# A written order for every operation in place of a planner: attention over memories and a gated feed-forward, one core

## The chip, the cores and the metric

The kernel runs on one core of a Trainium2 chip. A core has five engines with an instruction queue each: TensorE (PE, matrix products; its weight loads are shown apart as PEld), VectorE (DVE), ScalarE (ACT), GpSimd (POOL) and SyncE (SP, which here issues all transfers). Each queue is worked off in its own order; an instruction whose inputs or buffer are not ready holds everything behind it on that engine. The metric is the device time of one execution in microseconds (us).

## The reference

```
a = softmax(phi over seq)                      # batch 8, heads 8, seq 576, 32 memories
k_m = a^T k ; v_m = a^T v                      # 32 x 64 for each head
attn = softmax(q k_m^T / 8) ; y = attn v_m     # the heads of a token side by side: x, 4608 x 512
h = x @ w_in                                   # w_in 512 x 2048
g = h * erf(softplus(h))
out = g @ w_out                                # w_out 2048 x 512
```

Everything is float32, inputs and output.

## The kernel before, in words

The product `attn v_m w_in` is regrouped: `v_m w_in` is made first, per batch and per 256 columns of `w_in` (the tiles `vw` or `wv`), and `h` is then `attn` (the tiles `at`) times that. A step `i` is one of 128 pieces (batch `b`, 128 of the 2048 inner columns). Batches 0 and 1 make `h` with `ffn1` (L850, two halves of 288 tokens a step). Later batches take two steps at once with `quad` (L756, seven products in place of eight, with sums on DVE before and after). `h` comes out in PSUM as tiles `psh` and is copied or summed into SBUF by ACT or DVE: in batch 0 the copies may go to either engine (L864 on DVE, L865 on ACT), as may one of the four in a `quad` (L779 on DVE, L778 on ACT). Then ACT makes softplus (L872) and erf (L877), each after a table load when the function changes. DVE multiplies (L887), and the product is split into a rounded part (L903 on DVE or L904 on ACT) and the rest (L905 on DVE). From the two parts `ffn2` (L935, tile `g`) makes the second products, four groups of 128 tokens for each step, into the accumulators `pso`. The 64 tokens of a batch that are left over go through DRAM and are multiplied for two batches together (L935 into `psr`).

Most products use split operands, three matmuls for one; the first steps use plain float32. The small products of attention (L598 `phi` by `k`, `v`; L652 `q` by `km` and `w_in` by `vm`) use parts of the array. PSUM has four banks for all `psa` and `psh` tiles, and four for `pso`.

At the start the weights arrive packed and are decoded: DVE makes the upper half in place (L485, a CAST), ACT or DVE the lower half (L486 or L488), and DVE merges them (L480). `w_in` is needed for `vw`, `w_out` for the second products. A score tile `sc` goes through DVE and ACT (L798 transposition, L801 maximum, L803 difference, L806 exp, L807 sum, L809, L811, L812) and becomes `at` with L819. All transfers stand in one SP queue: `phiT`, `kv`, `q`, `w` (each packed weight chunk is one transfer), later `wi` and `rest_d`.

What sets the order of the instructions: every operation is recorded as an `Op` with an engine or two (`ways`), a modelled cost, a rank, and the operations that it must follow. `Plan.order()` then runs a small model of the engines. It takes at each moment the operation of lowest rank that can start soonest and whose tiles have room, with the shift of a table `SHIFT` added to some ranks, and chooses the engine where there are two. The result is the order of emission, and so the order in every queue. In the same model PE's waits of over 450 ns are filled with matmuls of zeros (`fill`, L414, tile `idle`) until the first operation of the kind "stop filling", which is the first second product of all:

```
if filling and gap > 450:
    x.fill = int((gap - 200) / (216 if clock.fast else 432))
...
op(PE, mm(DM, True) if exact else 3 * mm(DM, False), rank, gs + [w_key, o], [o], emit,
   kind="stop filling" if k == 0 else None)
```

Of the kernel before, what the change touches and what calls it, by code (L numbers as in the profile page):

```python
# [41 lines left out]
SHIFT = {  # L42
    "at_sums": {
        ("s", 2): 2, ("s", 3): 2,
    },
    "attention": {
        (0,): 12, (2,): 4.5, (3,): 1,
    },
    "decode": {
        ("in", 0): -9, ("in", 1): -10.5, ("in", 2): -12, ("in", 5): -11, ("in", 7): -11, ("out", 2): 11.5,  # L50
        ("out", 3): -14, ("out", 7): -0.5,
    },
    "ffn2_rest": {
        ("s", 0, 2): 5.5, ("s", 10, 2): -5.5, ("s", 12, 2): 3.5, ("s", 6, 2): 2, (7, 0, 2): -14,
    },
    "g_split": {
# [4 lines left out]
    },  # L61
    "memories": {
        (1,): 1.5, (2,): 4,
    },
    "split_wo": {
        (0,): 13, (4,): 4.5, (6,): 6,
    },
    "vw": {
        (0, 4, False): 1.5, (0, 6, False): -9.5, (1, 1, False): 0.5, (1, 5, False): 5, (1, 6, False): -5.5,
    },  # L70
    "vw_sums": {
        ("s", 3): -6.5, (2, 0): 8, (2, 1): 2.5, (2, 3): -1,
    },
}


class Op:
    def __init__(self, ways, rank, kind, nbytes, edge):
        self.ways, self.rank, self.kind, self.nbytes, self.edge = ways, rank, kind, nbytes, edge
        self.engine = next(iter(ways))  # L80
        self.before, self.after, self.tiles, self.placed = set(), [], set(), []
        self.ready = self.start = self.end = 0.0
        self.fill = 0
# [19 lines left out]

class Plan:
# [3 lines left out]
    SIGNAL = 60.0  # L108
    TABLE = 1283.0
    SWITCH = 98.0  # L110
    RELOAD = 170.0
    NEAR = 100.0

    def __init__(self, room, any_order, least, shared):
        self.ops, self.seen = [], {}
        self.room, self.any_order, self.least, self.shared = room, any_order, least, shared
        self.pool_of, self.users, self.turn = {}, {}, {}

    def tile(self, pool, *key):
        self.pool_of[key] = pool  # L120
        self.users[key] = []
        self.turn.setdefault(pool, []).append(key)
        return key

    shift = 0

    def op(self, engine, cost, rank, reads, writes, emit, kind=None, nbytes=0, edge=None, after=(),
           holds=(), other=()):
        x = Op({engine: (cost, emit), **dict(other)}, rank, kind, nbytes, edge)
        x.shift = self.shift  # L130
        x.before.update(after)
        for w, keys in ((False, reads), (True, writes)):
            for k in keys:
                k, part = (k[0], k[1]) if isinstance(k[0], tuple) else (k, None)
                x.tiles.add(k)
# [18 lines left out]
        for k in x.tiles:  # L154
            if k in self.users:
                self.users[k].append(x)
                x.placed.append(k)
        x.placed += [k for k in holds if k not in x.tiles]
# [3 lines left out]
    def order(self):  # L162
        n_wait = {}
        for x in self.ops:
            x.rank += 100 * x.shift
            n_wait[x] = len(x.before)
            for y in x.before:
                y.after.append(x)
        room, turn = dict(self.room), dict.fromkeys(self.turn, 0)
        left = {k: len(u) for k, u in self.users.items()}  # L170
        waiting = {e: [x for x in self.ops if e in x.ways and not n_wait[x]] for e in ENGINES}
        free = dict.fromkeys(ENGINES, 0.0)
        table, at_edge, small = None, True, False
        landed, clock, filling = 2200.0, Clock(), True
        releases, out, now, held = [], [], 0.0, set()

        def fits(x):
            need = {}
            for k in x.placed:
                if k in held:  # L180
                    continue
                p = self.pool_of[k]
                if p not in self.any_order and self.turn[p][turn[p] + need.get(p, 0)] != k:
                    return False
                need[p] = need.get(p, 0) + 1
            if any(room[p] < n for p, n in need.items()):
                return False
            return not any(p in self.least for p in need) or self.shared >= sum(
                max(n, self.room[p] - room[p] + need.get(p, 0)) for p, n in self.least.items())

        def best_way(x):
            return min(x.ways, key=lambda e: max(free[e], x.ready, now) + x.ways[e][0])

        while len(out) < len(self.ops):
            best = None
            for e, xs in waiting.items():
                can = [x for x in xs if fits(x)]
                if e == ACT and not at_edge:
                    can = [x for x in can if x.kind != "exp"]
                can = [x for x in can if len(x.ways) == 1 or best_way(x) == e]  # L200
                if not can:
                    continue
                t0 = max(free[e], now, min(x.ready for x in can))
                near = [x for x in can if x.ready <= t0 + self.NEAR]
                if e == PE and small and any(x.kind == "small" and x.ready <= t0 for x in near):
                    near = [x for x in near if x.kind == "small" and x.ready <= t0]
                x = min(near, key=lambda x: x.rank)
                t = max(free[e], x.ready, now)
                if best is None or t < best[0]:
                    best = (t, x, e)  # L210
            if releases and (best is None or releases[0][0] <= best[0]):
                now, _, p = heapq.heappop(releases)
                room[p] += 1
                continue
            if best is None:
                raise RuntimeError(f"nothing fits after {len(out)} of {len(self.ops)}")
            now, x, e = best
            x.engine, (cost, x.emit) = e, x.ways[e]
            for w in x.ways:
                waiting[w].remove(x)  # L220
            for k in x.placed:
                if k not in held:
                    held.add(k)
                    room[self.pool_of[k]] -= 1
                    turn[self.pool_of[k]] += 1
# [16 lines left out]
            elif e == ACT:  # L242
                if x.kind is not None and x.kind != table:
                    cost += self.TABLE
                    table = x.kind
                if x.edge is not None:
                    at_edge = x.edge
                late = 75.0
            elif e == DVE:
                late = 60.0  # L250
            x.cost = cost
            free[e] = now + cost
            x.start, x.end = now, now + cost + late
            if e == SP:
                begin = max(now + 900, landed)
                landed = begin + x.nbytes / (250 if x.nbytes < 1.2e5 else 340 if begin < 13000 else 385)
                x.end = landed + 900
            out.append(x)
            for y in x.after:
                n_wait[y] -= 1  # L260
                y.ready = max(y.ready, x.end + self.SIGNAL)
                if not n_wait[y]:
                    for w in y.ways:
                        waiting[w].append(y)
            for k in x.tiles:
                if k in left:
                    left[k] -= 1
                    if not left[k]:
                        end = max(u.end for u in self.users[k]) + self.SIGNAL
                        heapq.heappush(releases, (end, len(out) * 16 + len(releases), self.pool_of[k]))  # L270
# [4 lines left out]
def tile_memory_attention_then_erf_softplus_ffn(  # L275
# [12 lines left out]
    P = 128  # L288
# [21 lines left out]
    MOST = {"h": 14, "e": 12, "at": 14, "sc": 4, "phiT": 3, "uv": 3, "dk": 2, "rr": 3}  # L310
    LEAST = {"h": 4, "e": 4, "at": 7, "sc": 3, "phiT": 2, "uv": 1, "dk": 1, "rr": 2}
# [857 lines left out]
```

## Time and profile before

| | |
|---|---|
| three runs | 704.41 us median, 703.42 to 704.54 |
| the profiled execution | 704.14 us, its span 702.3 us |
| PE, PEld, DVE, ACT busy | 691.8, 549.8, 581.8, 541.9 us |
| HBM read and written | 93.2 and 21.0 MB |
| granted PE clock, mean | 0.998 |

A span is the time from the first to the last instruction; the execution is 1.8 us longer. Busy is the time in which an engine has at least one instruction in flight. Matmuls overlap, so PE's spacing is better read from a run of equal matmuls: its length over their count.

### The profile page before, as it was taken

The page shows a single profiled execution, that of the slowest core. Times are in us where ns is not written, and L with a number is a line of the kernel's source. Part 1 is how long each engine was busy: PE and PEld are TensorE (multiplying, and loading weights), DVE is VectorE, ACT ScalarE, POOL GpSimd, SP SyncE. Part 2 cuts the span into 40 slices and gives each one's busy share as a digit, 9 for nine tenths or more (in the row PEclk, how much of TensorE's full clock was granted, in tenths as well). Part 3 has the DMA queues.
Part 4 walks back from the last instruction along what each step waited for, and adds up shares of the span by engine and source line. Part 5 has one row for each costly group of instructions (what it writes and reads, how often), then busy time and mean ns, then how long its engine had stood idle before and what let it go on. Part 6 is the DMA issues. An engine that isn't in the chain of part 4 may idle for free.

```text
span 702.3 us, 13828 instructions
## 1 busy us (share of the span) xinstructions
PE 691.8 (99%) x5204; PEld 549.8 (78%) x5204; DVE 581.8 (83%) x1202; ACT 541.9 (77%) x978; POOL 30.6 (4%) x70
## 2 busy tenths in 40 slices
PE   8999999999999999999999999999999999999997
PEld 3566678778878888888878888788888888888885
DVE  3999999988878889998987997789998898767750
ACT  4689987977777887888878996589987895686831
POOL 0111210000000000000000000000000000011220
PEclk9999999999999999999999999999999999999999
DMA  8999953861736336273634346445321434330002
GB/s 324 415 393 421 378 186 105 289 238 34 256 106 214 102 123 227 76 236 91 250 119 139 99 147 229 128 133 191 117 76 66 122 100 139 98 110 1 1 1 75
DMA packets 71283, 115.07 MB, mean 164 GB/s; under 512 B 38064, under 2 KB 46256, under 8 KB 71216
## 3 DMA queue, kind: packets, MB, share of 16 engines
q1 hardware_dynamic: 71216, 114.18, 47.3%
q8 instruction: 41, 0.67, 0.4%
q14 instruction: 26, 0.21, 0.1%
HBM read 93.19 MB, written 20.97 MB: 163 GB/s over the span
## 4 chain that ended last, share of the span: by engine, by line
PE 90%; DMA 3%; DVE 3%; ACT 2%; SPq 1%; issue 1%; ACTq 0%; DVEq 0%
PE pso L935 48%; PE psh L756 19%; PE psh L850 7%; PE psr L935 6%; PE psa L652 6%; PE psa L598 2%; DMA q<-qT 2%; DMA phiT<-phiT 2%; PE idle L414 1%; DVE sv L677 1%; PE psa L620 0%; ACT wv L403 0%; SPq L442 0%; DVE wv L405 0%; DVE e L887 0%
## 5 line engine op out<-in xcount | busy, mean ns | idle before, releaser
L935 PE MATMUL pso<-wo,g 128*128 128x512 f32 x1440 | 392.6, 395 | 0.0
L935 PEld LDWEIGHTS pso<-wo,g 128*128 128x128 f32 x1440 | 250.4, 188 | 41.7 <-issue 7.3
L756 PEld LDWEIGHTS psh<-at,wv 128*128 128x128 f32 x1008 | 168.6, 188 | 36.5 <-DVE h L677 1.8
L756 PE MATMUL psh<-at,wv 128*128 128x288 f32 x1008 | 190.9, 298 | 1.2 <-ACT g L904 0.4
L872 ACT ACTIVATE e<-h 128x576 f32<-128x576 f32 x128 | 87.0, 685 | 38.8 <-DVE h L677 31.0
L887 DVE TENSOR_TENSOR e<-e,h 128x576 f32<-128x576 f32 x120 | 88.9, 749 | 19.7 <-ACT e L877 19.4
L905 DVE TENSOR_TENSOR g<-e,g 128x576 fp32r<-128x576 f32 x120 | 89.7, 750 | 0.6
L877 ACT ACTIVATE e<-e 128x576 f32<-128x576 f32 x128 | 84.1, 676 | 0.4
L677 DVE TENSOR_TENSOR uv<-uv,psh 128x288 f32<-128x288 f32 x96 | 43.1, 449 | 19.0 <-PE psh L756 15.8
L677 DVE TENSOR_TENSOR h<-uv,psh 128x288 f32<-128x288 f32 x96 | 43.1, 449 | 13.6 <-PE psh L756 13.0
L904 ACT ACTIVATE g<-e 128x576 fp32r<-128x576 f32 x68 | 46.5, 684 | 8.6 <-PE pso L935 4.1
L935 PE MATMUL psr<-wo,rr 128*128 128x512 f32 x192 | 49.5, 393 | 0.0
L850 PE MATMUL psh<-at_hi,vw 128*128 128x288 f32 x224 | 45.1, 306 | 0.8 <-DVE sc L798 0.8
L771 ACT ACTIVATE uv<-psh 128x288 f32<-128x288 f32 x96 | 38.9, 405 | 8.8 <-PE psh L756 8.0
L872 ACT ACT_TABLE_LOAD x33 | 42.3, 1283 | 3.9 <-DVE h L677 3.4
L877 ACT ACT_TABLE_LOAD x33 | 42.3, 1283 | 0.6
L935 PEld LDWEIGHTS psr<-wo,rr 128*128 128x128 f32 x192 | 34.8, 188 | 6.8 <-issue 0.4
L850 PEld LDWEIGHTS psh<-at_hi,vw 128*128 128x128 f32 x224 | 35.0, 188 | 5.9 <-issue 2.1
L914 POOL CAST rr<-g 128x64 fp32r<-128x64 f32 x32 | 14.0, 447 | 579.9 <-DVE g L903 550.6
L652 PE MATMUL psa<-wi,vm 64*32 64x256 f32 x1024 | 37.1, 383 | 0.0
L984 ACT ACTIVATE ot<-pso 128x512 f32<-128x512 f32 x32 | 18.5, 604 | 20.0 <-PE pso L935 19.7
L403 ACT ACTIVATE wv<-sv 128x512 fp32r<-128x512 f32 x48 | 27.8, 624 | 5.6 <-DVE sv L677 5.3
(88 smaller groups left out, 809.8 us busy)
## 6 DMA issues: line engine op xcount, KB each, us to landing
wi<-w_in_d SPq DMA_DIRECT2D x56, 512.0 KB, 4.6
kv<-kv SPq DMA_DIRECT2D x32, 640.0 KB, 9.1
q<-qT SPq DMA_DIRECT2D x16, 576.0 KB, 6.9
out<-ot SPq DMA_DIRECT2D x32, 256.0 KB, 3.5
w<-w_in SPq DMA_DIRECT2D x8, 1023.8 KB, 14.4
w<-w_out SPq DMA_DIRECT2D x8, 1023.8 KB, 13.6
rr<-rest_d SPq DMA_DIRECT2D x28, 256.0 KB, 3.4
rest_d<-g SPq DMA_DIRECT2D x104, 64.0 KB, 1.7
```

The costliest lines, as they stand in the source:

```text
L403: lambda: nc.scalar.activation(get_hi(), get_src(), AF.Identity))
L652: nc.tensor.matmul(out=get(ps[par])[p * M : (p + 1) * M, m * n : (m + 1) * n], lhsT=w[rows, p, :], rhs=get(x)[rows, p, :], start=True, sto ...
L677: op(DVE, on_dve(n) + extra, rank, reads, [o], lambda: nc.vector.tensor_tensor(out=get_o(), in0=get_x(), in1=get_y(), op=kind))
L756: nc.tensor.matmul(out=get(ps[o]), lhsT=lhsT, rhs=rhs, start=(n < 4 and m == 0), stop=(m == 2), skip_group_check=n >= 4)
L771: lambda x=x: nc.scalar.activation(get(uv)[:, x], get(ps[x]), AF.Identity))
L850: nc.tensor.matmul(out=get(ps), lhsT=x[:, g, k % 2 * P : (k % 2 + 1) * P], rhs=y[:, g, :], start=(n + g == 0), stop=(n == len(parts) - 1 a ...
L872: last[:] = [op(ACT, on_act(S), rank, [("h", i)], [e], lambda: nc.scalar.activation(get(e), get(("h", i)), AF.Softplus), kind="softplus", ...
L877: last[:] = [op(ACT, on_act(S), rank, [e], [e], lambda: nc.scalar.activation(get(e), get(e), AF.Erf), kind="erf", edge=edge, after=last)]
L887: op(DVE, on_dve(S), rank, [e, h], [to if i >= FR2 else (t, 0)], lambda: nc.vector.tensor_tensor(out=get(t)[:, 0].bitcast(F32) if i < FR2 ...
L904: other={ACT: (on_act(S), lambda: nc.scalar.activation(get(t)[:, 0], get(e), AF.Identity))})
L905: op(DVE, on_dve(S), rank, [e, (t, 0)], [(t, 1)], lambda: nc.vector.tensor_tensor(out=get(t)[:, 1], in0=get(e), in1=get(t)[:, 0].bitcast(F ...
L935: nc.tensor.matmul(out=o, lhsT=y, rhs=z, start=(start and n == 0), stop=(stop and n == len(parts) - 1))
```

## The change

The planner in `Plan.order()`, its tables of buffers and the table `SHIFT` go. In their place stands a string, `WRITTEN`, that spells 3504 numbers. The operations are recorded as before and sorted by rank. Each number `n` takes the operation at place `n >> 1` of those that are left, on its first or second engine by `n & 1`. The model of times remains only to decide where zeros are put, with three costs changed a little. The zeros no longer end at the first second product: "stop filling" now marks the second products of step 15. Zeros that stand behind the first second product would be added into the accumulator `pso` of batch 0 instead of being written into a tile of their own.

```diff
+WRITTEN = (
+    "KlcAAjCCAkOAIAEjMlGEACAheheAAAACAEEKACAKGACFDBAAAACAMMhIkcUMSiCSheSMhYhWaOMMWMUhUUhSUMAQeAOhEAAiCiCKCAIhahII"
...
+def numbers(text):
+    n = 0
+    for c in text:
+        d = DIGITS.index(c)
+        n = 32 * n + d % 32
+        if d < 32:
+            yield n
+            n = 0
...
     def order(self):
...
-                x = min(near, key=lambda x: x.rank)
-                t = max(free[e], x.ready, now)
...
+        left, out = sorted(self.ops, key=lambda x: x.rank), []
+        free, landed = dict.fromkeys(ENGINES, 0.0), 2200.0
+        clock, filling, small, table = Clock(), True, False, None
+        for n in numbers(WRITTEN):
+            x = left.pop(n >> 1)
+            e = list(x.ways)[n & 1]
+            cost, x.emit = x.ways[e]
+            now = max([free[e]] + [y.end for y in x.before])
...
     def mm(n, exact):
-        return 2 * (2 * n / 2.4 + 2.5) if exact else n / 2.4 + (15.5 if n == DM else 11.7)
+        return 2 * (2 * n / 2.4 + 2.5) if exact else n / 2.4 + (16.2 if n == DM else 12.3)
...
+        o = get(("pso", 0, 0)) if idle[1:] else idle[0] if idle else None
         for _ in range(n):
             nc.tensor.matmul(
-                out=idle[0].rearrange("p (n c) -> p n c", c=P), lhsT=zeros,
-                rhs=zeros.unsqueeze(1).to_broadcast([P, DM // P, P]), start=True, stop=True,
+                out=o.rearrange("p (n c) -> p n c", c=P), lhsT=zeros,
+                rhs=zeros.unsqueeze(1).to_broadcast([P, DM // P, P]),
+                start=not idle[1:], stop=not idle[1:], skip_group_check=len(idle) > 1,
             )
...
-           kind="stop filling" if k == 0 else None)
+           kind="stop filling" if i == NK - 1 else None)
```

The instructions are the same in kind and number but for a few. Copies of `psh` on ACT are 69 instead of 49, and on DVE 43 instead of 63: of the 20 that move, 11 are those of L864 and 9 those of L779. ACT has 64 instead of 68 of the copies of L904 and DVE has 56 instead of 52 of L903. Two of the decodes of L486 go from ACT to DVE (L488). ACT has 86 table loads instead of 84. The matmuls of zeros are 73 instead of 76; 70 of them stand ahead of the first `ffn1` and three behind its first 16 matmuls, and none behind the first second product.

Three places in the queues are shown. The first is SP's queue from its first transfer on. Before:

```order
L433 DMA phiT<-phiT 128x576 x2
L442 DMA kv<-kv 128x1280 x2
L447 DMA q<-qT 128x4x288
L428 DMA w<-w_in 128x4095
L442 DMA kv<-kv 128x1280 x2
L447 DMA q<-qT 128x4x288
L428 DMA w<-w_in 128x4095
L428 DMA w<-w_out 128x4095
L428 DMA w<-w_in 128x4095
L428 DMA w<-w_out 128x4095
```

And now, the lines being those of the changed kernel:

```order
L371 DMA phiT<-phiT 128x576 x2
L380 DMA kv<-kv 128x1280 x2
L385 DMA q<-qT 128x4x288
L366 DMA w<-w_in 128x4095
L385 DMA q<-qT 128x4x288
L366 DMA w<-w_in 128x4095
L380 DMA kv<-kv 128x1280 x2
L366 DMA w<-w_in 128x4095
L366 DMA w<-w_out 128x4095
L366 DMA w<-w_in 128x4095
```

The second pair of `kv` (for `v_m`) went behind the second `q` and the second `w_in`, and the third `w_in` stands ahead of the first `w_out`.

The second place is DVE's queue around the first `at` tile, with numbers that tell the tiles apart (`sc` with two numbers are the two halves of batch 0). Before, the first half's `at` comes first:

```order
L812 TENSOR_TENSOR sc_264<-sc_264,srs_375 128x576
L485 CAST w_124<-w_124 128x1024
L803 TENSOR_TENSOR sc_367<-sc_367,smx_377 128x576
L480 SCALAR_TENSOR_TENSOR wi_398<-w_124 128x1024
L807 TENSOR_REDUCE ssm_401<-sc_367 128x18
L485 CAST w_127<-w_127 128x1024
L485 CAST w_130<-w_130 128x1024
L809 TENSOR_SCALAR ssm_401<-ssm_401 128x18
L480 SCALAR_TENSOR_TENSOR wi_442<-w_130 128x1024
L811 RECIPROCAL srs_445<-ssm_401 128x18
L819 STREAM_TRANSPOSE at_479<-sc_264 128x576
L812 TENSOR_TENSOR sc_367<-sc_367,srs_445 128x576
```

Now the second half's comes first (`sc_292`):

```order
L748 RECIPROCAL srs_306<-ssm_295 128x18
L746 TENSOR_SCALAR ssm_304<-ssm_304 128x18
L418 SCALAR_TENSOR_TENSOR wi_375<-w_103 128x1024
L748 RECIPROCAL srs_379<-ssm_304 128x18
L418 SCALAR_TENSOR_TENSOR wi_381<-w_120 128x1024
L423 CAST w_135<-w_135 128x1024
L749 TENSOR_TENSOR sc_292<-sc_292,srs_379 128x576
L418 SCALAR_TENSOR_TENSOR wi_413<-w_135 128x1024
L756 STREAM_TRANSPOSE at_429<-sc_292 128x576
L749 TENSOR_TENSOR sc_254<-sc_254,srs_306 128x576
L341 TENSOR_TENSOR vw_458<-psa_443,vw_458 128x256
L756 STREAM_TRANSPOSE at_462<-sc_254 128x576
```

The same operations stand ahead of the first `at` in both, but for the CAST of the first `w_out` (`w_127`), which went behind both `at` tiles.

The third place is PE's queue in batch 5, where attention's small products of the next batch stand between the large ones. Before:

```order
L756 MATMUL psh<-at,wv 128x288 x3
L652 MATMUL psa<-q,km_98 32x288 x8
L756 MATMUL psh<-at,wv 128x288 x3
L935 MATMUL pso<-wo,g 128x512 x6
L652 MATMUL psa<-wi,vm_101 32x256 x16
L756 MATMUL psh<-at,wv 128x288 x3
L935 MATMUL pso<-wo,g 128x512 x3
```

Now:

```order
L694 MATMUL psh<-at,wv 128x288 x3
L872 MATMUL pso<-wo,g 128x512 x3
L590 MATMUL psa<-q,km_98 32x288 x8
L590 MATMUL psa<-wi,vm_101 32x256 x16
L694 MATMUL psh<-at,wv 128x288 x3
L872 MATMUL pso<-wo,g 128x512 x3
```

The two blocks of small products became one here; over the whole program they are 48 instead of 49.

## Rows read from the trace of the kernel before

**Rows 1.** The page's first part (busy time, share of the span, instructions) and the granted clock in 40 slices.

```profile
PE 691.8 (99%) x5204; PEld 549.8 (78%) x5204; DVE 581.8 (83%) x1202; ACT 541.9 (77%) x978; POOL 30.6 (4%) x70
PEclk9999999999999999999999999999999999999999
```

**Rows 2.** Busy time in stretches: the stretch, its length, busy time and instructions of each engine, granted clock, DMA share and GB/s.

```profile
14.30:17.60 3.30, 3.30 (x16) 1.37 (x14) 3.27 (x5) 1.80 (x1) 0.00 (x0) 1.00 1.05 394
17.60:19.40 1.80, 1.39 (x81) 1.18 (x81) 1.05 (x2) 1.02 (x3) 0.00 (x0) 1.00 1.04 419
...
31.00:100.00 69.00, 68.03 (x474) 44.88 (x475) 66.32 (x99) 61.56 (x98) 13.84 (x27) 1.00 0.97 367
100.00:703.00 603.00, 595.39 (x4402) 492.07 (x4400) 496.60 (x1069) 465.22 (x855) 13.98 (x32) 1.00 0.40 130
```

**Rows 3.** The chain that ended last, in order of time: start, length, what (x counts matmuls).

```profile
21.82 3.99 PE idle L414 x18
...
31.31 10.97 PE psh L850 x56
...
43.23 1.96 PE pso L935 x4
```

**Rows 4.** What PE waited for, by name, but for the three waits of the first 20 us: total us, times, longest.

```profile
PE pso L935 <- PE psh L850: 1.0, 1, 1.0
PE psh L850 <- DVE sc L798: 0.8, 1, 0.8
PE psh L756 <- ACT g L904: 0.4, 2, 0.2
...
PE psh L756 <- ACT bias L521: 0.3, 1, 0.3
PE psh L756 <- DVE wv L405: 0.3, 1, 0.3
```

**Rows 5.** The page's list of transfers: size of one, median us from issue to landing.

```profile
kv<-kv SPq DMA_DIRECT2D x32, 640.0 KB, 9.1
q<-qT SPq DMA_DIRECT2D x16, 576.0 KB, 6.9
...
w<-w_in SPq DMA_DIRECT2D x8, 1023.8 KB, 14.4
```

**Rows 6.** The first 45 us in order of time: start, length, engine, line, what, and in brackets the idle time before and what ended it.

```profile
13.60 0.85 DVE L798 STREAM_TRANSPOSE sc<-psa 128x288 f32<-128x288 f32 x2 [5.36 <-PE psa L652]
14.31 1.80 ACT L486 ACTIVATE w<-w 128x1024 int32<-128x1024 uint32 x1 [1.55 <-DMA w<-w_in]
...
17.66 1.33 PE L598 MATMUL psa<-kv,phi 116*32 116x64 f32 x80
...
20.54 0.57 ACT L634 ACTIVATE vm<-psa 64x128 f32<-64x128 f32 x2 [0.85 <-PE psa L620]
...
20.87 0.95 PE L652 MATMUL psa<-wi,vm 64*32 64x256 f32 x16
...
26.11 2.47 DVE L485 CAST w<-w 128x1024 f16<-128x1024 bf16 x2
...
27.04 2.49 ACT L486 ACTIVATE w<-w 128x1024 int32<-128x1024 uint32 x2
...
30.03 0.72 DVE L819 STREAM_TRANSPOSE at<-sc 128x576 f32<-128x576 f32 x1
...
31.15 7.92 PE L850 MATMUL psh<-at,vw 128*128 128x288 f32 x32
...
42.38 0.76 DVE L887 TENSOR_TENSOR g<-e,h 128x576 f32<-128x576 f32 x1
```

**Rows 7.** PE alone, in batch 5 and at the end.

```profile
481.60 0.72 PE L652 MATMUL psa<-q,km 64*32 64x288 f32 x16
482.24 0.66 PE L756 MATMUL psh<-at,wv 128*128 128x288 f32 x3
482.75 1.54 PE L935 MATMUL pso<-wo,g 128*128 128x512 f32 x6
484.22 1.09 PE L652 MATMUL psa<-wi,vm 64*32 64x256 f32 x32
485.24 0.67 PE L756 MATMUL psh<-at,wv 128*128 128x288 f32 x3
...
523.06 1.09 PE L652 MATMUL psa<-wi,vm 64*32 64x256 f32 x32
...
524.57 2.34 PE L935 MATMUL pso<-wo,g 128*128 128x512 f32 x9
```

**Rows 8.** Groups by line: count, busy us, mean ns of one, idle before it and what ended that.

```profile
L865 ACT ACTIVATE h<-psh 128x288 f32<-128x288 f32 x17 | 7.0, 413 | 5.3 <-PE psh L850 5.0
...
L872 ACT ACT_TABLE_LOAD x33 | 42.3, 1283 | 3.9 <-DVE h L677 3.4
L486 ACT ACTIVATE w<-w 128x1024 int32<-128x1024 uint32 x13 | 18.4, 1435 | 1.6 <-DMA w<-w_in 1.6
```

**Rows 9.** The last steps: the last copies and splits of `g` on DVE, and PE's last matmuls in the chain.

```profile
670.64 0.45 DVE L677 TENSOR_TENSOR h<-uv,psh 128x288 f32<-128x288 f32 x1
...
677.39 0.76 DVE L905 TENSOR_TENSOR g<-e,g 128x576 fp32r<-128x576 f32 x1
...
684.36 6.18 PE pso L935 x27
```

More of the change, by code (lines that the diff above doesn't have):

```diff
@@ L37, with __init__ @@
 }
[L42 to L56, printed above, removed]
[4 rows of a table removed]
[L61 to L74, printed above, removed]
-class Op:
[L78 to L83, printed above, removed]
+class Op:
+    def __init__(self, ways, rank, kind, nbytes):
+        self.ways, self.rank, self.kind, self.nbytes = ways, rank, kind, nbytes
+        self.before, self.end, self.fill = set(), 0.0, 0
 class Clock:
@@ L101, in to @@
         self.at = t
-class Plan:
[L108 to L114, printed above, removed]
-        self.ops, self.seen = [], {}
[L116 to L130, printed above, removed]
+DIGITS = "ABCDEFGHIJKLMNOPQRSTUVWXYZabcdefghijklmnopqrstuvwxyz0123456789+-"
@@ L131, in op, with __init__ @@
+def numbers(text):
[6 more added lines that the diff above has]
+            n = 0
+class Plan:
+    SIGNAL, TABLE, SWITCH, RELOAD = 60.0, 1283.0, 98.0, 170.0
+    def __init__(self):
+        self.ops, self.seen = [], {}
+    def op(self, engine, cost, rank, reads, writes, emit, kind=None, nbytes=0, after=(), other=()):
+        x = Op({engine: (cost, emit), **dict(other)}, rank, kind, nbytes)
         x.before.update(after)
@@ L162, in order @@
     def order(self):
[L163 to L206, printed above, removed]
-                x = min(near, key=lambda x: x.rank)
-                t = max(free[e], x.ready, now)
[L209 to L225, printed above, removed]
@@ L250, in order @@
                 late = 60.0
-            x.cost = cost
             free[e] = now + cost
-            x.start, x.end = now, now + cost + late
+            x.end = now + cost + late + self.SIGNAL
             if e == SP:
@@ L256, in order @@
                 landed = begin + x.nbytes / (250 if x.nbytes < 1.2e5 else 340 if begin < 13000 else 385)
-                x.end = landed + 900
+                x.end = landed + 900 + self.SIGNAL
             out.append(x)
[L259 to L270, printed above, removed]
+        assert not left
         return out
@@ L363, in tile_ @@
     def tile_(tag, *key, shape=None, dtype=F32, pool=None):
-        key = plan.tile(tag, *key)
         p, s, d = SHAPES.get(tag, (pool, shape, dtype))
         T[key] = lambda: pools[p].tile(
-            s, d, name=key[0], tag=tag if tag not in MOST else p, bufs=2 if tag == "rx" else None)
+            s, d, name=key[0], tag=p if tag in SHARED else tag, bufs=2 if tag == "rx" else None)
         return key
@@ L607, in one_memory @@
         cost = n_g * NC * (220 if b else 110)
-        op(PE, cost, rank, [a] + kvs, [ps], sums, kind="small", holds=[t])
+        op(PE, cost, rank, [a] + kvs, [ps], sums, kind="small")
         for n, g in enumerate(gs):
             rs = ("prs", b, g)
-            op(ACT, on_act(2 * n_x * D, True), rank, [ps, rs], [(t, n)],
+            op(ACT, on_act(2 * n_x * D, True) + 70, rank, [ps, rs], [(t, n)],
                lambda n=n, rs=rs: nc.scalar.activation(
@@ L760, in product @@
             chain[:] = [op(PE, 3 * mm(U, False), rank + (0 if n < 4 else 60) + 0.1 * n,
-               [(w, (m, a_part)) for m in range(2)] + [at_] + ([] if n < 4 else [ps[o]]), [ps[o]], emit,
-               holds=h + [uv] if n == 0 else (), after=chain)]
+               [(w, (m, a_part)) for m in range(2)] + [at_] + ([] if n < 4 else [ps[o]]), [ps[o]], emit, after=chain)]
         def half(r, u):
@@ L948, in emit @@
         def emit():
+            if i == d == 0:
+                idle.extend([None] * (2 - len(idle)))
             w = [wf[k // 2][:, k % 2]] if exact else [get(w_key)[:, x, k % 2] for x in range(2)]
```

126 lines of the change are left out of this document (77 added, 49 removed), and 4 rows, old and new, of the table SHIFT.

## The prediction, made before the changed kernel ran

> **What bounds the kernel now.** I read the busy time first, then the chain of waits, then the stretches, and the order of time at the start and at the end. The busy time shows TensorE at 99%, ScalarE at 77%, VectorE at 83%, and a granted clock of 1.00 (2.4 GHz) in practically every slice [rows 1]. A busy PE need not be a PE at its pace, so I check the spacing: 27 second products late in the program take 6.18 us, 229 ns each [rows 9], where 512 columns at 2.4 GHz are 213 ns. After the first 31 us PE waits by name only 2.8 us in all: 1.0 once, 0.8 once, and five waits of 0.2 or 0.3 [rows 4]. So nearly every microsecond after the start is a matmul that must be made. An order can only move three things: when the large matmuls begin, what PE waits for behind that, and how often it changes between large and small products.
>
> At the start the chain goes through matmuls of zeros; the large products begin at 31.3 us, run 10.97 us, and the first second product comes at 43.23 after a pause of about a microsecond [rows 3]. In those 31 us PE does little that counts; transfers and VectorE set the pace.
>
> By the Trainium skill (Perfetto Trace Analysis, Identifying the Most-Contended Engine) busy matmuls are a bad measure and the share of weight loads is a better one; that share is 78% here [rows 1] and would leave a fifth of the span as headroom. The spacing of 229 ns against 213 bears out much less, some 7%. By the page a new order could win far more than I allow; it is the fourth rival below.
>
> **Part 1: the first large product (-1.55 us).** Two things are moved. On SP the `kv` pair goes behind a `q` and a `w_in`, and the third `w_in` goes ahead of the first `w_out`. The transfers run at about 0.41 MB per us there (394 and 419 GB/s, DMA share over 1) [rows 2], with 1.31 MB for the `kv` pair, 0.59 for `q` and 1.05 for a weight chunk [rows 5]. The `kv` pair comes (0.59 + 1.05)/0.41 = 4.0 us later than at 17.66 [rows 6], at 21.7. The third `w_in` comes 1.05/0.41 = 2.6 us earlier than at 27.04 [rows 6], at 24.5. On ACT its decode now stands between the `kvk` and the `vm` copies.
>
> The path by `vm`: the decode takes 24.5 to 25.9 (1.44 us [rows 8]); the copies of `vm` follow, and the first product by `w_in` comes 0.33 us after they start (20.54 to 20.87 [rows 6]), at 26.2. Two blocks in a row take 1.6 us, ACT empties their four banks by 28.4, the third block takes 0.7, and the first `ffn1` can start at about 29.2.
>
> The path by `at`: from the first score transposition at 13.60 to the end of the first `at` at 30.75 VectorE needs 17.15 us [rows 6]. The new queue has the same operations ahead of it but one CAST of 1.24 us (2.47 for two [rows 6]), which now stands behind both `at` tiles: 15.9 us, so 29.5, and 29.9 with the 0.4 us that lie between `at` and the first matmul now. The second `at` comes about 2 us later (a product, a split of `vw`, a transposition), within the 3.9 us that half of the 7.92 us block gives it.
>
> So it starts between 29.2 and 29.9 instead of 31.15; I take 29.6. If the third `w_in` comes no earlier than 27.04, its cast, two products and the transposition (1.3 + 0.7 + 1.2 + 0.7) end at 30.9 and nothing is won: bound 0. The other bound is -1.95.
>
> **Part 2: from there to the first second product (-0.35 us).** It takes 12.1 us now (31.15 to 43.23), of which PE works 10.97 [rows 3]; the rest is a wait for the first `g` tile, whose product starts at 42.38 [rows 6]. In the new ACT queue no weight decode stands between the copies of `h` and the first erf; one did (1.44 us [rows 8]). What PE does is the same plus three matmuls of zeros, 0.22 us each (3.99/18 [rows 3]): 11.65 us. That is the lower end, so the gain lies between 0.45 and 0 us; I take 0.35. The zeros stand beside the wait and cost nothing; without that cover they cost 0.65.
>
> **Part 3: one change of products fewer (-0.25 us).** `q` alone takes 0.64 us to the next large matmul, two blocks of `w_in` 1.02, together 1.66; the three in one take 1.51 [rows 7]. The three large matmuls behind a block take 0.51 us (482.24 to 482.75) where their columns need 0.36. So 0.15 + 0.1.
>
> **Part 4: the waits behind 100 us (-0.45 us).** There are 1.8 us of them [rows 4], where PE needs a PSUM bank that ScalarE or VectorE has not yet emptied. All could go (-1.8), or others of that size could come (+1.8). The places where small products come are nearly the same, often with 3 to 6 second products behind them where 6 to 9 stood, so new waits are as likely as old ones are removed. VectorE's load falls by 20 copies, which makes a bank a little sooner free: I let a quarter go.
>
> **Part 5: what costs nothing.** The 20 copies that go to ACT and two more table loads (1.283 us each [rows 8]) lie beside PE: ScalarE is busy 465 us of the 603 behind 100 us [rows 2]. The Trainium skill (ScalarE: Activation LUTs, Table sets: the hidden batching unit) asks to do all calls of one set before changing. By it the two loads would cost 2.57 us, and the sum would come out at no change; the row's 1283 ns agrees with the page's price, but the idle time covers it.
>
> The zeros change nothing by the clock, which is granted in full already. The end has cover too. Before, the last split of `g` comes 7.5 us after the last sum into `h` starts (670.64 to 678.15) and PE then still has 19 us of work [rows 9]. Now 66 second products stand behind the last first product, 15.1 us at 229 ns, and the last two `g` tiles are needed after 42 of them, 9.6 us. So the same chain ends 2.1 us ahead of its use. If it does not, each microsecond is one at the end.
>
> **The sum.** -1.55 - 0.35 - 0.25 - 0.45 = -2.6 us. On the profiled execution, 702.3 of span and 1.8 around it, 704.14, that makes 701.54. It lies 0.27 under the median shown, so the prediction is 704.41 - 2.6 = 701.8.
>
> **The rivals.**
>
> *The gain at the start is given back (703 to 704.6; point 703.8).* Between 31 and 100 us the DMA share is 0.97 [rows 2], with most weight chunks still to come. If PE runs ahead by 1.9 us, it meets a chunk or the first tiles of batch 1 that come when they came before, and waits. Then only parts 3 and 4 remain: 704.41 - 0.7 = 703.7. For it: the full transfers. Against it: behind 20 us no wait on a transfer stands in PE's list [rows 4], so there is some lead now. Chance 0.2.
>
> *ScalarE holds the softplus back (705.5).* 11 of the copies moved to ACT are of the first 16 steps, in the stretch where ScalarE is busy 61.56 of 69 us [rows 2]. They cost 11 x 0.41 = 4.5 us less two decodes of 1.44, so 1.7 net, and 5.7 us of idle time remain. But a copy that stands ahead of its matmul holds all behind it: the present copies there waited 5.0 us for PE [rows 8], six times, 0.83 each. If all 11 wait so, that is 9.1 us, 3.4 more than is there, and the second products of batch 0 come that late: 704.41 - 2.3 + 3.4 = 705.5. It decides from a mean wait of 0.73 us on, (5.7 + 2.3)/11. Against it: counted by the mean durations of the rows, what stands ahead of each `g` tile on ScalarE and VectorE is no longer than before at nearly every step. Chance 0.11, up to 709.
>
> *The zeros do not do what they say.* None of the 73 stands behind the first second product, so that half of the change has no effect here; the time is then that of the forecast, which counts them only in part 2.
>
> *The waits all go and PE draws together (700).* With all 1.8 us of part 4 and the best of parts 1 and 2: 704.41 - 1.95 - 0.45 - 0.25 - 1.8 = 700. Chance 0.11.
>
> **How the numbers follow.** The forecast has 0.58, with its own range of 700.8 to 703. What a measurement of this kernel can tell from no change is 0.2%, 1.4 us: faster means under 703.0, slower over 705.8. Faster: 0.58 + 0.11 and a little of the first rival, 0.70. Same: most of the first rival and the better half of the second, 0.20. Slower: 0.10. The range of 699.7 to 704.8 holds the forecast, the first rival and most of the last; the second lies outside.
>
> **What would show it.** Step 1: the first `ffn1` at 29.2 to 29.9 us, the `kv` wait at 21.7, the third decode at 24.5. Step 2: the first second product 11.7 us later, with at most a short wait. Part 4: PE's named waits behind 100 us, 1.8 before. End: no wait of PE in the last 30 us. A start at 31 us, named waits on transfers between 40 and 100 us, or PE waiting on `g` with ACT copies ahead of it would prove the forecast wrong.

## The result and the profile after

The changed kernel is slower: 710.59 us (median of 5 runs, 709.21 to 713.57) against 704.54 (5 runs, 703.42 to 706.75), a ratio of 1.0087 (95% interval 1.0058 to 1.0117). Forecast were 701.8 us and a range of 699.7 to 704.8: faster was forecast, and it is slower. The profiled execution has a span of 708.5 us where 702.3 stood, 6.2 more.

The page's first part and its clock row, against [rows 1]:

```profile
PE 691.7 (98%) x5201; PEld 553.8 (78%) x5201; DVE 581.4 (82%) x1187; ACT 539.9 (76%) x995; POOL 26.2 (4%) x70
...
PEclk9999899999999999999999999999999999999999
```

PE's busy time is the same in sum, so the time in which it stands has grown by 6.3 us. The one 8 in the clock row, the fifth slice (71 to 89 us), shows where to look. What PE waited for by name, against [rows 4] (total us, times, longest):

```profile
PE pso L872 <- DVE g L824: 5.2, 2, 5.1
PE psa L536 <- DMA kv<-kv: 1.6, 1, 1.6
PE psa L590 <- DMA wi<-w_in_d: 1.3, 2, 0.8
PE psh L787 <- ACT h L802: 1.1, 1, 1.1
PE psh L787 <- DVE vw L341: 1.1, 1, 1.1
```

One wait of 5.1 us for a `g` outweighs all others. The timeline around it (start, length, engine, line, what, and in brackets the idle time before and what ended it):

```profile
71.06 0.19 POOL L364 MEMSET w<- 128x1 uint16 x2 [18.50 <-DMA w<-w_out]
...
71.28 1.22 DVE L418 SCALAR_TENSOR_TENSOR wi<-w 128x1024 uint32<-128x1024 uint32 x1 [8.89 <-POOL w L364]
...
72.82 0.75 DVE L824 TENSOR_TENSOR g<-e,h 128x576 f32<-128x576 f32 x1
...
73.62 2.08 PE L872 MATMUL pso<-w,g 128*128 128x512 f32 x2 [5.07 <-DVE g L824]
```

Read backwards, this is a chain over four queues. PE waits for the `g` of step 5. VectorE makes it late because the instruction three places ahead, the merge of a `w_in` chunk, waited 8.89 us. The merge waited for a MEMSET on POOL that takes 0.1 us. And POOL had stood 18.5 us before two MEMSETs, until a `w_out` chunk had landed. These are the MEMSETs of `load_weight`: a packed chunk is transferred as 4095 columns, and POOL clears the 4096th. The written order puts them so (POOL's queue, with numbers; `w_732` is the sixth `w_out` chunk, `w_434` the seventh `w_in` chunk):

```
L364 MEMSET w_668 128x1
L835 TENSOR_TENSOR rx_644<-g_633,rx_644 128x64
L364 MEMSET w_732 128x1
L364 MEMSET w_434 128x1
L834 CAST rx_740<-g_603 128x64
L835 TENSOR_TENSOR rx_740<-g_603,rx_740 128x64
```

The list has the MEMSET of `w_732` one place behind that chunk's own transfer (places 239 and 238). That transfer was issued at 59.67 us, when the merge of an older chunk had left its buffer, and took 11.24 us. `w_434`, behind it, had no reason to wait.

SP, which issues all transfers, stood behind the same MEMSET too. Its transfer of the left-over tokens (`rest_d`) needs the `rx` that POOL makes behind it, and SP issued nothing between 60.5 and 72.7 us. SP's waits for `rx` over the whole run, in the changed kernel and in the one before:

```profile
SPq L846 <- POOL rx L835: 31.0, 4, 12.1
```

```profile
SPq L909 <- POOL rx L898: 2.1, 3, 0.9
```

The price does not end with the wait. The stretches around it (length, busy time of PE, PEld, DVE, ACT, POOL, granted clock, DMA share, GB/s):

```profile
70.00:72.00 2.00, 0.00 (x0) 0.00 (x0) 0.72 (x1) 0.00 (x0) 0.86 (x4) 0.79 0.77 319
72.00:74.00 2.00, 0.38 (x1) 0.38 (x2) 2.00 (x5) 0.00 (x0) 0.68 (x1) 0.50 0.17 45
74.00:76.00 2.00, 2.00 (x5) 0.97 (x5) 2.00 (x6) 0.00 (x0) 1.26 (x3) 0.50 1.10 328
76.00:78.00 2.00, 2.00 (x10) 2.00 (x10) 1.97 (x4) 0.00 (x0) 0.00 (x0) 0.50 0.96 258
78.00:80.00 2.00, 2.00 (x59) 1.43 (x61) 0.53 (x3) 0.95 (x3) 0.00 (x0) 1.00 0.92 303
```

After PE had stood since 68.5 us, the granted clock fell to 0.50 (1.2 GHz) and came back at about 78. The chain has second products (`pso`) and first products (`psh`) at both levels of the clock:

```profile
44.22 4.49 PE pso L872 x10
48.71 3.18 PE psh L787 x24
...
73.62 2.08 PE pso L872 x2
75.70 2.67 PE psh L787 x12
```

Two second and twelve first products took the 4.75 us from 73.62 to 78.37; at the pace of the two rows above they need 2.5. So 2.3 us are lost in slow matmuls.

The start, against [rows 3] and [rows 6], came out better than forecast:

```profile
22.11 1.30 PE psa L536 x80
23.42 0.02 issue
23.44 0.62 ACT kvk L550 x2
24.07 1.67 ACT w L424
...
28.82 7.97 PE psh L787 x32
...
40.79 2.84 PE pso L872 x6
```

The first large product begins 2.4 to 2.5 us sooner (28.82 against 31.31 in the chain, 28.75 against 31.15 in the timeline), and the first second product, at 40.79 instead of 43.23, keeps that lead. One trace does not give this to better than about 1 us: in the seven traces with this order and these queues at the start (this one and six of the runs below) the first large product begins at 27.8 to 29.2 us, each time 18.8 us behind the first `kv` product, which comes when its transfer lands, at 8.9 to 10.4. In the two traces with the start of before it begins at 31.15 and 30.06.

Add it up: -2.4 at the start, +1.1 (PE waiting for a copy of `h` at 65.8), +5.1, +2.3, and behind 100 us waits by name of 2.8 instead of 1.8, +1.0. That is +7.1; 6.2 were measured. The difference of 0.9 us is within what the start moves from one execution to the next.

### The profile page after: what moved, and what is told of

It is laid out like the page before. It is cut to its first block, busy times and chain, and to the rows that moved or that the text cites. A ratio compares the mean times of both kernels' runs of the same rounds, so it can differ in the third digit from the quotient of the medians.

```text
span 708.5 us, 13745 instructions
## 1 busy us (share of the span) xinstructions
PE 691.7 (98%) x5201; PEld 553.8 (78%) x5201; DVE 581.4 (82%) x1187; ACT 539.9 (76%) x995; POOL 26.2 (4%) x70
## 4 chain that ended last, share of the span: by engine, by line
PE 85%; DMA 6%; DVE 4%; ACT 2%; SPq 1%; issue 1%; POOL 0%; DVEq 0%; POOLq 0%; ACTq 0%
PE pso L872 45%; PE psh L694 18%; PE psh L787 6%; PE psr L872 6%; PE psa L590 5%; PE psa L536 2%; DMA w<-w_out 2%; PE idle L351 1%; DMA kv<-kv 1%; DMA phi<-phi 1%; DMA wi<-w_in_d 1%; DMA rest_d<-g 1%; DMA q<-qT 1%; ACT e L814 1%; ACT L814 1%
## 5 line engine op out<-in xcount | busy, mean ns | idle before, releaser
L872 PE MATMUL pso<-wo,g 128*128 128x512 f32 x1440 | 388.6, 395 | 0.0
L809 ACT ACTIVATE e<-h 128x576 f32<-128x576 f32 x128 | 85.0, 681 | 17.8 <-DVE h L615 15.8
L841 ACT ACTIVATE g<-e 128x576 fp32r<-128x576 f32 x64 | 43.5, 682 | 16.0 <-PE pso L872 4.9
L339 ACT ACTIVATE wv<-psa 128x256 fp32r<-128x256 f32 (+1 forms) x96 | 28.8, 336 | 22.2 <-PE psa L590 20.5
L341 DVE TENSOR_TENSOR wv<-psa,wv 128x128 fp32r<-128x128 f32 (+1 forms) x96 | 32.1, 347 | 5.0 <-ACT wv L339 4.9
L872 PE MATMUL pso<-w,g 128*128 128x512 f32 x64 | 30.6, 616 | 5.2 <-DVE g L824 5.2
```

What stands on the lines that cost most here:

```text
L341: lambda: nc.vector.tensor_tensor(out=get_lo(), in0=get_src(), in1=get_hi().bitcast(F32), op=ALU.subtract))
L809: last[:] = [op(ACT, on_act(S), rank, [("h", i)], [e], lambda: nc.scalar.activation(get(e), get(("h", i)), AF.Softplus), kind="softplus", ...
L841: other={ACT: (on_act(S), lambda: nc.scalar.activation(get(t)[:, 0], get(e), AF.Identity))})
L872: nc.tensor.matmul(out=o, lhsT=y, rhs=z, start=(start and n == 0), stop=(stop and n == len(parts) - 1))
```

## The experiments

All edits stand at the end of `order()`, where `out` is the written order and its index the place of an operation; `fill` is the number of zeros ahead of a matmul. Each time is the median of its runs, with the ratio to the kernel before measured beside it; the kernel before took 703.7 us in the first set, 704.17 in the second, 704.08 in the third.

### One MEMSET moved

```diff
         assert not left
+        out.insert(239, out.pop(243))
         return out
```

> The changed kernel with one instruction moved: POOL's MEMSET of the last column of the seventh w_in chunk goes ahead of the MEMSET for the sixth w_out chunk; nothing else moves. Theory M (a queue behind a wait that no data asks for): in the changed kernel the w_out MEMSET waits on POOL until that chunk's transfer has landed (70.9 us), the w_in MEMSET behind it holds a merge on VectorE for 8.9 us, and PE waits 5.07 us for g at 68.5 and then works at a granted clock below 1 for two second and twelve first products (4.68 us where 2.45 are needed, 2.2 us lost). With the swap VectorE's wait of 8.9 us and PE's of 5.07 go, the clock between 60 and 80 us is 1.00, and the time is 710.6 - 5.07 - 2.2 = 703.3 us (702.5 to 704.2). Theory T (transfers: the early start only meets chunks that come when they come): the wait moves to the next tile that hangs on a transfer, PE waits over 3 us elsewhere between 60 and 100 us, and the time stays at 708 or above.

Measured: 709.39 us, ratio 1.0084 (1.0057 to 1.0110). Neither theory as it was put. The merge ran on time, at 61.59 us; and then VectorE stood again. Its longest wait between 55 and 80 us, first of the changed kernel, then of this one:

```profile
DVE wi L418 <- POOL w L364: 8.9, 1, 8.9
```

```profile
DVE g L825 <- POOL rx L836: 7.5, 1, 7.5
```

The wait moved, but not to a transfer's tile: the same `g` now waits 7.5 us for POOL's `rx` of step 2, which stands behind the MEMSET too. There are three buffers for `g`; step 5 takes that of step 2, and POOL had not read it yet. Two victims stood in one queue, and with the first one freed the second still costs PE the same (5.3 us, longest 5.1). SP is held as before, 10.9 us for the `rx`.

### The MEMSET ahead of its own transfer

```diff
+        out[238], out[239] = out[239], out[238]
```

> The changed kernel with the MEMSET for the sixth w_out chunk put just ahead of that chunk's own transfer; the w_in MEMSET stays behind it on POOL. Theory M, in the form that the MEMSET waits for the transfer because it stands behind it: now it waits only until its buffer is free, which is when the merge at 58.42 us is done (59.7 us), the w_in MEMSET follows at once, and the merge on VectorE (due at 62.4) waits for nothing: 703.3 us as with the swap. If the MEMSET is late for another reason (POOL itself, or the buffer), it still runs at 71 us and the time stays at 710.6.

Measured: 702.64 us, ratio 0.9991 (0.9972 to 1.0010). POOL:

```profile
59.10 0.19 POOL L365 MEMSET w<- 128x1 uint16 x2 [7.25 <-DVE wi L419]
59.30 0.24 POOL L835 CAST rx<-g 128x64 fp32r<-128x64 f32 x1
```

The MEMSET runs at 59.1 us, when the merge has left the buffer, and not at 71. PE's longest wait behind 31 us is 1.0, and the clock between 60 and 80 us is 1.00. One swap of neighbours is worth 7 to 8 us (6.8 by the two ratios, 8.0 by the two medians). So the MEMSET behind its transfer waited for the whole of it, though they touch different columns.

### Both victims ahead, the MEMSET left waiting

```diff
+        out[239:247] = [out[i] for i in (243, 244, 246, 239, 240, 241, 242, 245)]
```

> The changed kernel with three POOL instructions moved ahead of the MEMSET for the sixth w_out chunk: the MEMSET of the seventh w_in chunk and the CAST and TENSOR_TENSOR that make the left-over tokens of step 2 (rx) from g. That MEMSET itself stays behind its own transfer. With the w_in MEMSET alone moved, VectorE's 8.9 us at the merge went, but it then waited 7.5 us ahead of the g of step 5 for those rx instructions, since that g takes the buffer of step 2's. If these two instructions behind the waiting MEMSET are all that it costs, the MEMSET may wait until 70 us and nobody notices: VectorE has no wait on POOL, PE none on g over 0.4 us, and the time is that of the kernel whose MEMSET stands ahead of its transfer, 702.6 us (701.5 to 704). If something else that hangs on the chunk is late as well, the time stays at 705 or above.

Measured: 702.11 us, ratio 0.9977 (0.9959 to 0.9995), the first of the two readings. The wait is there, and costs nothing:

```profile
69.90 0.10 POOL L365 MEMSET w<- 128x1 uint16 x1 [14.36 <-DMA w<-w_out]
```

With the run before, this settles the cause: the late chunk itself hurts nobody; what hurts is what stands behind its MEMSET. SP is freed here too, since it waits for the `rx`; no run frees SP alone, so its share in the price is not known.

### The same swap the other way, in the kernel before

There the MEMSET of the sixth `w_out` chunk stands ahead of its transfer; this run puts another one, of the eighth `w_in` chunk, behind its own.

```diff
+        out[227], out[228] = out[228], out[227]
```

> The kernel before with one thing added: on POOL the MEMSET for the eighth w_in chunk (57.9 us) goes behind that chunk's own transfer (issued at 58.0 us). Theory M: it now waits until the chunk has landed, 9 to 12 us later; behind it on POOL stand the MEMSET of the seventh w_out chunk, whose transfer (63.4) moves to 68 us or later, and the rx instructions of steps 2 and 3 (63.1), whose g buffers VectorE wants at 70.5. VectorE waits on POOL for up to 1 us, the last two w_out chunks come 5 us later, and the time is 705 to 709 us. If a MEMSET waits for no transfer but only for its buffer, it runs at 58 us as before and the time is that of the kernel before.

Measured: 703.5 us, ratio 0.9991 (0.9978 to 1.0004): no price. The mechanism is there, since the MEMSET went from 57.91 to 67.47 us and the `rx` with it:

```profile
67.47 0.22 POOL L427 MEMSET w<- 128x1 uint16 x2 [21.58 <-DVE prs L546]
67.63 1.14 POOL L898 CAST rx<-g 128x64 fp32r<-128x64 f32 x2
68.84 1.14 POOL L899 TENSOR_TENSOR rx<-g,rx 128x64 fp32r<-128x64 f32 x2
```

(The name in the bracket is the last event that the profile saw, long past.) But the `g` that needs the buffers came at 70.5 us before, 0.5 after `rx` was done here (VectorE waits 0.2 us for it), and SP's wait of 5.4 us for a MEMSET ahead of the next weight chunk cost nothing that can be measured. The expected 705 to 709 us was wrong: I had priced the delay of the queue, and not the slack of those behind it.

### Zeros in the wait

```diff
+        out[280].fill = 22
```

> The changed kernel with 22 matmuls of zeros (22 x 0.216 = 4.75 us) put into PE's wait of 5.07 us, in front of the first second product of step 5; the wait itself stays. If the 2.2 us that PE loses behind the wait are the price of its idleness (the granted clock 0.83 between 60 and 80 us), they come back: clock 1.00, wait by name under 0.4 us, and 710.6 - 2.2 = 708.4 us. If the slow matmuls behind the wait have another cause (the weight chunk, the accumulator), they stay slow and the time is 710.6.

Measured: 711.74 us, ratio 1.0109 (1.0087 to 1.0132): no better than the changed kernel. The clock theory holds and the 2.2 us do not come:

```profile
60.00:80.00 20.00, 17.84 (x161) 10.62 (x163) 10.82 (x20) 10.43 (x19) 2.81 (x7) 1.00 0.90 335
```

```profile
74.01 1.13 PE L873 MATMUL pso<-w,g 128*128 128x512 f32 x2 [0.24 <-DVE g L825]
...
107.90 0.79 PE L591 MATMUL psa<-wi,vm 64*32 64x256 f32 x16 [2.15 <-DMA wi<-w_in_d]
```

The zeros kept the clock at 1.00, and the products behind the wait run at their pace. But VectorE, 9 us behind its own work, now sets the pace at three places (waits of 0.2 to 0.4 us), and at 105.75 us PE meets a `wi` transfer and waits 2.15 us where the changed kernel waited 0.49. Its waits for `wi` are the larger part: 3.9 us in all where the changed kernel had 1.3.

```profile
PE psa L591 <- DMA wi<-w_in_d: 3.9, 2, 2.1
```

So PE, ahead by what the zeros gave back, met tiles that were late all the same.

### No zeros at all

```diff
+        out.insert(239, out.pop(243))
+        for x in out:
+            x.fill = 0
```

> The kernel with the one MEMSET moved, and without any matmul of zeros (73 fewer). What the zeros are worth: if PE's clock is granted in full without them, the time is that of the kernel with the MEMSET moved, 703.3 us (the zeros stand only where PE waits). If idleness costs PE its clock as behind the 5 us wait, the stretch from 13 to 45 us has a granted clock well below 1 and the first 32 large products take up to twice 7.97 us: the time is 2 to 8 us more, 705 to 711 us.

Measured: 712.1 us, ratio 1.0113 (1.0090 to 1.0136), against 1.0084 with the same MEMSET moved: 0.3%, 2 us, at the low end of what was expected, and the two intervals overlap, so a price at the end is not shown. (The base of the expectation was wrong too: that kernel takes 709.4, not 703.3.) At the start the traces differ clearly:

```profile
9.50 2.36 PE L539 MATMUL psa<-kv,phi 116*32 116x64 f32 x80 [0.69 <-ACT phi L517]
...
29.90 10.17 PE L790 MATMUL psh<-at,vw 128*128 128x288 f32 x32
```

The first 32 large products take 10.17 us instead of 7.97, the first nine of them at half the pace (4.59 us, 0.51 each), and 80 small products at the start 2.36 instead of 1.33. The granted clock says 1.00 in both stretches; why the products are slower there, no row says.

### The start undone

```diff
+        out[238], out[239] = out[239], out[238]
+        out[11:21] = [out[i] for i in (15, 17, 11, 12, 13, 14, 16, 18, 20, 19)]
```

> The kernel with the MEMSET ahead of its own transfer (702.6 us), with the first seven weight, kv and q transfers in the order of before: the kv pair for v_m ahead of the second q and the second w_in, the first w_out ahead of the third w_in. Everything else stays. If the start's gain comes from the order of transfers and reaches the end, the first large product goes from 28.1 us back to 30.5 to 31.2 and the time is 702.6 + 2.4 to 3.0 = 705.0 to 705.6. If it comes from VectorE's queue alone (the CAST of w_out behind both at), the start stays under 29.5 us and the time at 702.6. If transfers between 31 and 100 us take an early start back, the first product is late and the time is 702.6 to 703.3 all the same.

Measured: 707.0 us, ratio 1.0046 (1.0029 to 1.0063), 0.55% and 0.69%, 4 to 5 us, above the two kernels that cure the wait. The chain:

```profile
18.56 1.21 PE psa L592 x16
19.77 6.50 PE idle L353 x25
26.27 1.26 PE psa L538 x80
...
32.70 7.97 PE psh L789 x32
```

The first large product comes at 32.7 us, later than before the change (31.3): the second score block has to wait for `q` until 18.56, and 25 zeros and the `kv` product stand behind it. About 1 us of it is the clock, which was granted at 0.59 and 0.56 from 18 to 22 us, behind PE's wait of 2.9: the 25 zeros took 6.50 us where they take 5.50. So the start's gain needs the new order of the transfers, to which the queues of the engines are fitted, and a later start reaches the end whole. Whether the transfers alone, with the queues of before, would win it was not run.

### The copies back to VectorE

This leaves the written places as they are and gives 26 copies of `psh` the engine they had before.

```diff
+        out[238], out[239] = out[239], out[238]
+        for i in (108, 111, 121, 130, 155, 159, 195, 258, 271, 272, 275, 286, 291, 319, 327, 1204, 1425, 1596, 1941,
+                  1984, 2091, 2285, 2340, 2826, 2868, 2971):
+            out[i].emit = next(f for _, f in out[i].ways.values() if f is not out[i].emit)
```

> The kernel with the MEMSET ahead of its own transfer (702.6 us), with every copy of psh that may go to either engine on the engine that had it before (23 copies from ScalarE to VectorE, 3 the other way), at the same places of the written order. By the prediction's part 5 the copies cost nothing on ScalarE: the time is 702.6, within 0.7 us. By the rival that ScalarE holds softplus back, taking 11 of them out of the first 16 steps pays: 701.5 or less. If VectorE is the tighter of the two in the first 16 steps, it costs: 704 or more, with PE waiting on VectorE for h or vw.

Measured: 704.37 us, ratio 1.0002 (0.9990 to 1.0015), 0.1% to 0.25% above the two cured kernels: 0.8 to 1.8 us, with an interval that overlaps both of theirs. So taking the copies off ScalarE does not pay, and a gain from having them there is not shown. The chain from 28.5 us on goes through VectorE (`DVE w`, `DVE h`, `DVE at_lo`) where it went through PE and ScalarE, but PE's longest waits in this trace are for transfers (1.6 us for `q`, 1.5 for `wi`), not for VectorE.

### Two repairs

```diff
+        out[238], out[239] = out[239], out[238]
+        out.insert(389, out.pop(402))
+        out.insert(299, out.pop(376))
+        out[80:84] = [out[i] for i in (81, 82, 83, 80)]
+        out[84].fill, out[95].fill = 2, 5
```

The first repair is the last two lines (ScalarE's order and the zeros), the second the two inserts (SP's order).

> The kernel with the MEMSET ahead of its own transfer (702.6 us), with two repairs of waits that its trace still shows. On ScalarE the two copies of vm go ahead of the decode of the third w_in (1.61 us on the chain at 23.47), with 2 and 5 zeros where 8 and 3 stood: the first large product comes at 27.6 us instead of 28.1. On SP the write of a decoded w_in chunk (issued at 88.9 us) goes ahead by some 15 us and the load of batch 1's third w_in ahead of two rest_d and three phiT transfers: PE's wait of 1.0 us at 98 us goes. If both hold, 702.6 - 0.5 - 1.0 = 701.1 us. If the start is bound by the landing of kv and the third w_in rather than by ScalarE's order, the first part gives 0; if the load waits for its buffer, the second does.

Measured: 699.23 us, ratio 0.9931 (0.9911 to 0.9951): the fastest of all, 4.9 us under the kernel before and 11 under the changed one. It was more than expected, so each repair ran alone.

> The kernel with the MEMSET ahead of its own transfer, with the first of the two repairs alone: ScalarE's two copies of vm ahead of the decode of the third w_in, 2 and 5 zeros where 8 and 3 stood. The kernel without repairs took 702.6 us in one set of runs, and one with the same queues but for three POOL instructions 702.1 in another; both repairs together 699.2. If the chain at 23 to 28 us is bound by ScalarE's order, the first large product comes 0.5 us sooner and the time is 701.6 to 702.1. If the repairs do more together than their waits (1.5 us) because of this one, it is under 701; if the start hangs on the landing of kv and w_in, 702.6.

Measured: 700.89 us, ratio 0.9962 (0.9942 to 0.9982).

> The kernel with the MEMSET ahead of its own transfer, with the second repair alone: on SP the write of a decoded w_in chunk some 15 us sooner and the load of batch 1's third w_in ahead of five transfers. If the load's late issue makes the wait of 1.0 us at 98 us, the wait goes and the time is 701.1 to 701.6. If it waits for its buffer or the line of transfers, the wait stays and the time is 702.1 to 702.6.

Measured: 701.32 us, ratio 0.9963 (0.9947 to 0.9979). The two do their part alone, some 0.15% to 0.3% each by these ratios, and together about the sum. With the second alone PE's wait of 1.0 us at 98 us is gone, as expected. With the first alone the large products begin at 27.27 us, and in the trace with both at 30.09:

```profile
27.27 8.01 PE psh L790 x32
```

```profile
30.09 8.01 PE psh L792 x32
```

The second trace is of the slowest execution of its six (701.36 us). Its first `kv` product came 1.6 us later, at 10.39, and the clock was granted at 0.50 from 12 to 14 us. So the gain of the first repair at the start rests on one trace.

## Why the prediction was wrong

**The step that failed** is not a term of the sum but the list of what an order can move: "when the large matmuls begin, what PE waits for behind that, and how often it changes". What PE waits for was priced in part 4 alone, from the waits that stood in the profile before, 1.8 us behind 100 us, with a bound of the same size upwards. Between the first second product (43 us) and 100 us the sum has no term for a wait at all. A new order can make a wait that no row of before has: the runs showed 5.1 us for `g` there and 2.3 us of slow matmuls behind it. It came from POOL, 4% busy, whose queue the prediction never read: it followed SP, PE, DVE and ACT. The rows to ask stood in the trace of before. POOL's MEMSETs stood there, by the profile's list, 27.8 and 14.1 us in all for `w` transfers, and no compute engine waited for them; only SP did:

```profile
SPq L428 <- POOL w L426: 12.5, 3, 6.4
```

Such a wait costs nothing as long as what stands behind it in the queue is not needed. The new queue put a MEMSET that a merge needed and an `rx` behind it.

**Part 1** (-1.55 taken, -2.4 measured) was right in mechanism and, in this trace, beyond its own bound of -1.95. The mis-sized term is VectorE's path: 17.15 us less one CAST was taken as work. It held waits, 0.75 us for `sc` from ScalarE and 0.39 for the score block of the late `q` among them; with `q` ahead of `kv` the block came at 15.9 instead of 19.4 and these waits went. `at` was done at 28.1 where 29.5 was worked out. The path by `vm`, which then set the start, gave 28.8 where 29.2 was worked out. The landing of `kv` (22.1 against 21.7 forecast) and the third decode (24.07 against 24.5) fit.

**Part 2** (-0.35 taken): from the first large to the first second product 12.04 us by the timeline (28.75 to 40.79), against 12.08 before: nothing, the upper end of its bounds. The wait for the first `g` shrank to 0.2 us, but the products and zeros ahead of it took 11.9 us and not 11.65.

**Parts 3 and 4** (-0.7 together): the waits behind 100 us grew from 1.8 to 2.8 us in the changed kernel; in the trace with the MEMSET ahead of its transfer they were 0.6, in the one with both victims moved 2.7. The products' blocks were not measured apart. (The prediction counts five waits of 0.2 or 0.3 us behind 31 us; the rows have four, and the sum of 2.8 us is right.)

**Part 5**: that the tail costs nothing holds (PE has no wait in the last 30 us), though two readings of it were wrong. The last split of `g` before the change is one at 685.64 us, which had waited 7.0 us for PE, and not the one that ends at 678.15; and 72 products stand behind the last first product, not 66. That the 20 copies cost nothing agrees with the run that moves them back; the two table loads were not tested alone. That the clock "is granted in full already" was no proof that zeros do nothing: without them the first 32 large products take 2.2 us more.

**The rivals.** "The gain at the start is given back" came nearest in what one would see, a wait between 40 and 100 us that ends with a transfer; its mechanism is refuted, since the chunk lands as late in the run with both victims moved, at no price, and since the start's gain reaches the end. "ScalarE holds the softplus back" shows once, the 1.1 us at 65.8, with two exponentials (0.77 and 1.26 us) just ahead of the copy; moving the copies off it does not pay. "All waits go" has the time of the repaired kernel, 699.2 against its 700, but not by its way: PE's waits behind 100 us are 1.7 us in that trace. With the wait cured the forecast's -2.6 us (0.9963) stands against 0.9991 (0.9972 to 1.0010), which cannot be told from no change, and 0.9977 (0.9959 to 0.9995), which is faster, with 0.9963 inside its interval. So the wait is 6.8 to 7.7 us of the error of 8.8, by the ratios; whether a part of the gain is missing for another reason stays open.

## What to carry to other kernels

Before an order is priced, walk every queue that it touches, the idle ones first: for each instruction that waits for something late, list what now stands behind it and when that is needed. A wait that costs nothing in the old trace is not harmless: it is covered by the order, and a new order can take the cover away. And when a wait is cured and the time stays, look for the next victim in the same queue before giving up the theory: the first repair here changed next to nothing, and the queue was the cause.

## What was not expected of the hardware

A MEMSET of one column, 0.1 us of work, did not start before a transfer into the other 4095 columns of its tile had landed (71.06 us, 11.4 after the issue of that transfer; POOL had stood 18.5 us by then); placed ahead of the transfer it ran at 59.1 us, when the buffer was free. PE's granted clock was 1.00 until 70 us, fell to 0.50 after it had stood since 68.5, and was 1.00 again from 78, with the work there taking 4.75 us instead of 2.5. Giving the clock back with zeros won nothing in this place. And in the kernel without zeros the granted clock reads 1.00 while 32 equal matmuls take 10.17 us instead of 7.97: read the lengths beside it.
